# State-read stores in another shape, alpha's copy on another engine, three weight loads issued later, other warm-up counts and a new table of slots

## The chip, the cores and the metric

The kernel runs on one core of a Trainium2 chip. The metric is the device time of one execution in microseconds (us), less being better; the number given for a kernel is the median of several runs. A profile of one execution is taken beside them. Its span runs from the first to the last instruction that the profiler recorded, and the device time of that execution is a little longer than the span. The engines are called PE (TensorE), DVE (VectorE), ACT (ScalarE), POOL (GpSimd) and SP (SyncE); PEld is the weight load of TensorE.

## What is computed

Eight batches with eight heads each. A head has 512 tokens of width 64 (x) and 32 state rows of width 64. Tokens read from the state and the state reads from the tokens, and both results go through a feed-forward block with a sine activation.

```python
scores  = scale * x @ state.T            # 512 x 32 per head
a       = softmax(scores)                # over the state rows
xread   = a @ state                      # 512 x 64
scores2 = scale * state @ x.T            # 32 x 512
a2      = softmax(scores2)               # over the tokens
sread   = a2 @ x                         # 32 x 64
y       = concat([xread, sread])         # 544 rows per batch, heads side by side: 512 wide
h       = y @ w_in                       # 512 -> 2048
g       = h + sin(alpha * h)**2 / (alpha + 1e-9)
out     = g @ w_out                      # 2048 -> 512
```

All inputs and the output are fp32; the kernel multiplies in bf16.

## The kernel before

**Main idea.** The token reads are not formed. The kernel multiplies the state with w_in first (M, 256 rows of state and head by 2048), and then h is A times M, with A the normalised weights. One Exp serves both softmaxes: E = exp(scores), its row sums (R) normalise A, its column sums (C, made by a matmul with ones) normalise the state reads. The state reads of all eight batches are gathered in `xs_all`, 256 rows, and go through the feed-forward block as a ninth stage.

**Stages and slots.** The main loop has nine stages t (eight batches, then the state reads) of 16 slots f, one for each 128 columns of the 2048. A slot does, in this order: `mm1` (two matmuls of 512 columns into a PSUM buffer `h_ps`, then Sin on ACT, then the square s*s on POOL, or on DVE if the slot is listed in `SQ`); the PE work of the attention that the table puts there; `snake` of the slot two earlier on DVE (s2 / alpha + h, which makes `gT` and frees the PSUM buffer, of which there are four); the DVE squares that are due; some second matmuls `mm2` of the stage before, as many as `TWO0`, `TWO1` or `TWO` say; and then the work of other engines that the table puts there. So PE alternates between the first product of batch t and the second of batch t-1. When 16 second matmuls have filled a tile of 128 rows, ACT copies it out and SP stores it.

**The table.** `BATCH` says for batch 0, 1, 2 and all later ones in which slot each step of that batch's attention stands, counted from the start of the stage before its own (for M and W from its own stage): L the load of x, P the two packs of x, T its transpose, S scores, X Exp, R row sums, N the two scalings that make A, A its transpose, M the four quarters of M with `MA` saying whether ACT (1) or DVE (0) casts each half, W the state reads. `ND` lists which scalings run on DVE; others run on POOL. The order of the program is the order on each engine: nothing is reordered, and each engine waits in its own queue.

**Transposes.** For batches 0 and 1 PE transposes x and A (`T`, `AT_`) and DVE or ACT copies the result from PSUM. For later batches SP issues transposing DMAs (`T_dma`, `AT_dma`), which stand in SP's queue among the output stores.

**Start.** SP loads the state and the x of batch 0. POOL makes an identity, waits for the state (`held`), and then issues the casting loads: the four quarters of w_in ('i'), the four of w_out ('o') and the x of batch 1 in the order `LOADS`. PE runs `warm_up` matmuls, transposes the state (`prep_state`) and alpha (`prep_alpha`), and then goes through batch 0's attention: T, S, the first quarter of M (`m_step(0, 0)`), W and Cs, warm-ups again, and `AT_`.

**End.** The state reads of 256 rows give two output tiles. `store` writes a tile of state reads as 4 batches by 32 rows. The second tile is done in halves of 256 columns by `mm2_last`: ACT copies the first half, DVE the second, and each is stored on its own.

Of the kernel before, what the change touches and what calls it, by code (L numbers as in the profile page):

```python
# [12 lines left out]
BF16 = mybir.dt.bfloat16  # L13
# [6 lines left out]

BATCH = {0: {'M': (-11, 0, 6, 8), 'MA': ((1, 0), (1, 1), (1, 0), (1, 1))},
 1: {'P': (0, 1),
     'T': (3, 3),
     'S': (3, 3),
     'X': (3, 3),
     'R': (3, 7),
     'N': (8, 10),
     'A': 13,  # L30
     'M': (-6, 0, 3, 9),
     'MA': ((1, 1), (1, 1), (1, 1), (0, 1)),
     'W': (5, 5)},
 2: {'L': -8,
     'P': (-1, -1),
     'T': 1,
     'S': (6, 6),
     'X': (6, 6),
     'R': (7, 8),
     'N': (7, 11),  # L40
     'A': 11,
     'M': (-5, -2, 5, 10),
     'MA': ((1, 1), (1, 1), (1, 1), (0, 1)),
     'W': (-1, -1)},
 3: {'L': -18,
     'P': (-12, -11),
     'T': -6,
     'S': (2, 2),
     'X': (2, 2),
     'R': (3, 4),  # L50
     'N': (3, 9),
     'A': 12,
     'M': (-3, 1, 6, 8),
     'MA': ((1, 0), (1, 0), (0, 1), (1, 1)),
     'W': (-2, -2)}}

SQ = {0: (4, 8, 9, 11, 12, 15),
 1: (3, 6, 11, 12, 14),
 2: (0, 2, 5, 10, 11, 14),
 7: (0, 1, 2, 3, 4, 5, 8, 10, 12),  # L60
 8: (0, 1, 2, 3, 4, 8, 9, 11, 12, 14)}
ND = {1: (), 2: (0,), 3: (0,)}
XS0 = 0

TWO0 = (0, 0, 0, 0, 0, 4, 3, 1, 0, 0, 1, 6, 1, 2, 3, 0)
TWO1 = (2, 4, 2, 1, 1, 2, 3, 2, 5, 3, 9, 3, 0, 3, 3, 0)
TWO = (7, 3, 4, 7, 0, 6, 11, 5, 4, 1, 0, 6, 2, 4, 1, 3)
WARM = (8, 3)

LOADS = ('i0', 'i1', 'x1', 'i2', 'o0', 'o1', 'i3', 'o2', 'o3')  # L70


@with_exitstack
def kernel(
# [9 lines left out]
    nc = tc.nc  # L84

    B, H, S, D = x.shape
    Ns = state.shape[2]
    P = nc.NUM_PARTITIONS
    C = S // P
    Q = H // 2  # L90
    G = 2
    HH = H // G
    TB = S + Ns
# [7 lines left out]
    const = ctx.enter_context(tc.tile_pool(name="const", bufs=1))  # L101
# [35 lines left out]
    def load_x(b, parts):  # L137
        xnat = xpool.tile([P, H, C * D], BF16, name="xnat")
        xv = x[b].rearrange("h (p i) d -> p h (i d)", i=C)
        hs = H // parts  # L140
        for k in range(parts):
            nc.gpsimd.dma_start(
                xnat[:, k * hs:(k + 1) * hs, :], xv[:, k * hs:(k + 1) * hs, :]
            )
        xnat_l[b] = xnat
# [8 lines left out]
    w_in_sb = wpool.tile([P, Q, DFF], BF16, name="w_in_sb")  # L154
    w_in_v = moe_w_in.rearrange("(q p) f -> p q f", p=P)
    w_out_sb = wpool.tile([P, FT, DOUT], BF16, name="w_out_sb")
    w_out_v = moe_w_out.rearrange("(ft p) c -> p ft c", p=P)
    for what, k in LOADS:
        k = int(k)
        if what == "x":  # L160
            load_x(k, 1)
        elif what == "i":
            cols = slice(k * FW, (k + 1) * FW)
            nc.gpsimd.dma_start(w_in_sb[:, :, cols], w_in_v[:, :, cols])
        else:
            fts = slice(k * 4, (k + 1) * 4)
            nc.gpsimd.dma_start(w_out_sb[:, fts, :], w_out_v[:, fts, :])

    ones = const.tile([P, D], BF16, name="ones")
    nc.vector.memset(ones[:], 1.0)  # L170
# [5 lines left out]
    nc.vector.memset(stT[:].bitcast(U32), 0)  # L176
    alpha_sb = const.tile([P, FT], FP32, name="alpha_sb")
    inva_sb = const.tile([P, FT], FP32, name="inva_sb")
    xs_all = const.tile([P, Q, B * Ns], BF16, name="xs_all")

    def warm_up(n):
        if n:
            wp = psO.tile([P, S], FP32, name="o_ps", tag="o")
        for _ in range(n):
            nc.tensor.matmul(wp[:], warm[:, 0:P], warm[:], start=True, stop=True)

    def kind(t):
        return t if t < 2 or t >= B - 1 else 2


    def prep_state():
        st2 = const.tile([P, 16, 2, D], BF16, name="st2")
        for half, copy in ((0, nc.vector.tensor_copy), (1, nc.scalar.copy)):
            js = slice(half * 8, (half + 1) * 8)
            copy(st2[:, js], st_nat[:, js].unsqueeze(2).to_broadcast([P, 8, 2, D]))
        for half in range(2):
            tp = psH.tile([P, 8, P], BF16, name="st_ps", tag="h")
            for k in range(8):
                nc.tensor.transpose(
                    tp[:, k, :],  # L200
                    st2[:, half * 8 + k].rearrange("p r d -> p (r d)"),
                    ident[:],
                )
            for r in range(2):
                rows = slice(r * D, (r + 1) * D)
                src = tp[rows].rearrange("d k (e r2 jh) -> d e r2 jh k", r2=2, jh=2)
                dst = stT[rows].rearrange(
                    "d bg (h2 r2 jh hf k) -> d (bg h2) r2 jh hf k", h2=2, r2=2, jh=2, hf=2
                )
                nc.scalar.copy(dst[:, :, r, :, half, :], src[:, :, r])  # L210

    def prep_alpha():
        tp = psH.tile([P, FT], FP32, name="al_ps", tag="h")
        nc.tensor.transpose(tp[:], alpha_rows[:], ident_f[:])
        nc.vector.tensor_copy(alpha_sb[:], tp[:])


    class Att:
# [81 lines left out]
                    ALU.mult,  # L300
                )

        def AT_(a, gs, copy=nc.vector.tensor_copy):
            tp = psX.tile([P, len(gs), S], BF16, name="a_ps", tag="px")
            for k, g in enumerate(gs):
                for i in range(C):
                    nc.tensor.transpose(
                        tp[:, k, i * P:(i + 1) * P], a.A[:, g, i], ident[:]
                    )
            copy(a.AT[:, gs[0]:gs[-1] + 1, :], tp[:])  # L310

        def W(a, pool=psX, tag="px"):
            a.wc = pool.tile([P, Q, 3 * Ns], FP32, name="w_ps", tag=tag)
# [20 lines left out]
        def xs(a):  # L334
            rC = smallp.tile([P, Q, Ns], FP32, name="rC")
            nc.vector.reciprocal(rC[:], a.wc[:, :, 2 * Ns:])  # L336
            for r in range(2):
                rows = slice(r * D, (r + 1) * D)
                nc.vector.tensor_tensor(
                    xs_all[rows, :, a.b * Ns:(a.b + 1) * Ns],  # L340
                    a.wc[rows, :, r * Ns:(r + 1) * Ns],
                    rC[rows],
                    ALU.mult,
                )

# [29 lines left out]
    def mm1(t, f):  # L375
        n = S if t < B else B * Ns
        hp = psH.tile([P, S], FP32, name="h_ps", tag="h")
        if t < B:
            for g in range(G):
                nc.tensor.matmul(  # L380
                    hp[:, :n], Ms[t][:, g, f * P:(f + 1) * P], atts[t].AT[:, g, :],
                    start=(g == 0), stop=(g == G - 1),
                )
        else:
            for q in range(Q):
                nc.tensor.matmul(  # L386
                    hp[:, :n], w_in_sb[:, q, f * P:(f + 1) * P], xs_all[:, q, :],
                    start=(q == 0), stop=(q == Q - 1),
                )
        s = sinp.tile([P, S], BF16, name="s")  # L390
        nc.scalar.activation(s[:, :n], hp[:, :n], ACT.Sin, scale=alpha_sb[:, f:f + 1])  # L391
        s2 = sinp.tile([P, S], BF16, name="s2")
        if f in SQ[kind(t)]:
            late.append((s2, s, n))
        else:
            nc.gpsimd.tensor_tensor(s2[:, :n], s[:, :n], s[:, :n], ALU.mult)  # L396
        return hp, s2, n
# [26 lines left out]
    def store(t, st, o_sb, cols, eng):  # L424
        if t < B:
            r0 = t * TB + st
            eng.dma_start(out[r0:r0 + C * (P - 1) + 1:C, cols], o_sb[:, cols])
        else:
            n = P // Ns
            ov = out.rearrange("(b t) c -> b t c", t=TB)  # L430
            eng.dma_start(ov[st * n:(st + 1) * n, S:, cols], o_sb[:, cols])


    def mm2_last(t, st):
# [18 lines left out]

    warm_up(WARM[0])
    prep_state()
    prep_alpha()
    a = atts[0] = Att(0)
    a.alloc()
    a.pack(0)
    a.pack(1)  # L460
    a.T(0)
    a.T(1)
    a.S(0)
    a.X(0)
    a.S(1)
    a.X(1)
    a.Rs(0)
    a.N(0, nc.gpsimd)
    a.Rs(1)
    a.N(1, nc.vector)  # L470
    m_step(0, 0, (True, True))
    a.W(psO, "o")
    a.Cs()
    warm_up(WARM[1])
    nc.scalar.activation(tiny[:, 1:2], warm[:, 0:1], ACT.Sin)
    a.AT_([0], nc.scalar.copy)
    a.AT_([1])
    nc.vector.tensor_scalar(inva_sb[:], alpha_sb[:], 1e-9, None, op0=ALU.add)
    nc.vector.reciprocal(inva_sb[:], inva_sb[:])
# [15 lines left out]
    for b in range(B):  # L495
        p = BATCH[min(b, 3)]
        s0 = (b - 1) * FT
        if b > 1:
            add(post, s0 + p["L"], load_x, b, 1)
        if b:  # L500
# [8 lines left out]
            for g in range(G):  # L509
                add(pe, s0 + p["S"][g], att, b, "S", g)  # L510
                add(post, s0 + p["X"][g], att, b, "X", g)
                add(post, s0 + p["R"][g], att, b, "Rs", g)
                eng = nc.vector if g in ND[min(b, 3)] else nc.gpsimd
                add(post, s0 + p["N"][g], att, b, "N", g, eng)
# [17 lines left out]
    todo = [(0, st, ft, ft + 1) for ft in range(FT) for st in (0, 1)]  # L532
    rows(0, TWO0, todo)
    todo += [(0, st, ft, ft + 1) for st in (2, 3) for ft in range(FT)]
    rows(1, TWO1, todo)
    assert not todo
    for t in range(2, B + 1):
        todo = [(t - 1, st, ft, ft + 1) for st in range(C) for ft in range(FT)]
        rows(t, TWO if t < B - 1 else (4,) * FT, todo)

# [21 lines left out]
    n = B * Ns // P  # L562
# [31 lines left out]
```

## Time and profile before

The time before is 238.24 us, the median of 13 runs from 236.59 to 240.8 us. The profiled execution took 238.24 us as well.

| quantity | value |
|---|---|
| profiled execution, device time | 238.24 us |
| its span | 236.2 us |
| mean granted TensorE clock | 0.978 |
| PE busy | 216.6 us, 92% |
| DVE busy | 178.5 us, 76% |
| ACT busy | 163.2 us, 69% |
| POOL busy | 108.5 us, 46% |
| first `mm1` matmul starts | 16.79 us |
| last matmul ends | 229.0 us |

Busy time is the sum of instructions on an engine. For PE it includes the time a result needs to come out of the array, so that a PE that is busy need not be at its peak: one 512-column matmul of `mm1` is listed with 0.38 us, while one follows the other every 0.216 us. In the lists of groups, each row has a line of the kernel, an engine, an operation with its output and input, a count, and then busy time, the mean of one in ns, and the idle time of the engine before it with what ended it. The chain of waits is followed back from the last instruction, at each step to what released it.

### The profile page before, as it was taken

Reading aid. Unit: us, or ns where it says so; the run is one execution under the profiler, and the core shown is the slowest. Engines: PE = TensorE matmul, PEld = TensorE weight load, DVE = VectorE, ACT = ScalarE, POOL = GpSimd, SP = SyncE. Lnnn points to the kernel's source line nnn. Section 1 sums busy time; section 2 is a strip of 40 time slices with the busy share of each in tenths; the row PEclk is TensorE's granted clock in tenths of the full one; section 3 lists DMA queues with packets and bytes.
Section 4 is the critical chain, followed back from the end, with each engine's and each line's share of the span. In section 5 each row is a group of like instructions: output and inputs, shape, how many; then the busy total and the mean of one; then the engine's idle time right before and its main releaser. Section 6 shows DMA issues by size and latency. Waiting matters only on the chain.

```text
span 236.2 us, 4158 instructions
## 1 busy us (share of the span) xinstructions
PE 216.6 (92%) x1505; PEld 104.0 (44%) x1532; DVE 178.5 (76%) x315; ACT 163.2 (69%) x264; POOL 108.5 (46%) x116
## 2 busy tenths in 40 slices
PE   7587797899999999999999999999999999999970
PEld 2444242444544444444444344444444444656550
DVE  3669998998886989788988798788779876644300
ACT  4559976898796679767976597759776676554310
POOL 3936577538337634573358316731671044231200
PEclk9959999999999999999999999999999999999996
DMA  7999996807811781178119902710231111111211
GB/s 219 188 198 201 206 142 75 191 13 179 133 45 46 178 136 44 44 182 130 49 44 154 159 0 92 177 45 4 89 89 47 44 46 44 49 46 57 79 22 67
DMA packets 36578, 23.35 MB, mean 99 GB/s; under 512 B 19645, under 2 KB 32205, under 8 KB 36557
## 3 DMA queue, kind: packets, MB, share of 16 engines
q0 software_dynamic: 11504, 7.87, 23.7%
q1 hardware_dynamic: 25020, 15.21, 22.5%
q8 instruction: 12, 0.20, 0.3%
q14 instruction: 10, 0.07, 0.1%
q10 hardware_dynamic: 32, 0.01, 0.0%
HBM read 17.31 MB, written 8.91 MB: 111 GB/s over the span
## 4 chain that ended last, share of the span: by engine, by line
PE 75%; DMA 10%; DVE 7%; issue 2%; ACT 1%; POOL 1%; ACTq 0%
PE o_ps L415 44%; PE h_ps L380 19%; PE m_ps L361 4%; DMA xnat<-in_x_dram 3%; PE h_ps L386 3%; DMA w_in_sb<-in_moe_w_in_dram 3%; DVE gT L406 3%; DMA AT<-A 2%; DMA st_nat<-in_state_dram 2%; PE o_ps L440 1%; PE w_ps L316 1%; PE s_ps L271 1%; PE w_ps L327 1%; DVE xp L234 1%; DVE rC L336 1%
## 5 line engine op out<-in xcount | busy, mean ns | idle before, releaser
L396 POOL TENSOR_TENSOR s<-s 128x512 bf16<-128x512 bf16 (+1 forms) x84 | 85.4, 1023 | 109.5 <-ACT s L391 104.5
L415 PE MATMUL o_ps<-w_out_sb,gT 128*128 128x512 bf16 x508 | 130.7, 380 | 1.4 <-issue 0.8
L391 ACT ACTIVATE s<-h_ps,alpha_sb 128x512 bf16<-128x512 f32 (+1 forms) x144 | 93.8, 669 | 50.5 <-PE h_ps L380 37.1
L406 DVE SCALAR_TENSOR_TENSOR gT<-s,inva_sb,h_ps 128x512 bf16<-128x512 bf16 (+1 forms) x144 | 99.8, 712 | 21.8 <-POOL s L396 20.5
L380 PE MATMUL h_ps<-AT,M 128*128 128x512 bf16 x250 | 73.1, 381 | 4.3 <-DVE gT L406 2.7
L415 PEld LDWEIGHTS <-gT 128*128 128x128 bf16 x528 | 49.0, 98 | 57.0 <-issue 6.4
L380 PEld LDWEIGHTS <-M 128*128 128x128 bf16 x256 | 24.6, 98 | 34.0 <-issue 5.5
L403 DVE TENSOR_TENSOR s<-s 128x512 bf16<-128x512 bf16 (+1 forms) x60 | 25.5, 435 | 5.1 <-ACT s L391 4.8
L370 ACT CAST M<-m_ps 128x512 bf16<-128x512 f32 x46 | 25.5, 589 | 1.2 <-PE m_ps L361 1.2
L421 ACT COPY o_sb<-o_ps 128x512 f32<-128x512 f32 x33 | 19.6, 594 | 4.9 <-PE o_ps L415 4.7
L372 DVE CAST M<-m_ps 128x512 bf16<-128x512 f32 x18 | 12.3, 685 | 4.8 <-PE m_ps L361 4.8
L361 PE MATMUL m_ps<-w_in_sb,stT 64*32 64x512 bf16 x256 | 13.3, 393 | 1.5 <-DMA w_in_sb<-in_moe_w_in_dram 1.2
L284 DVE TENSOR_REDUCE R<-E 128x16 f32<-128x512 bf16 x16 | 10.9, 682 | 2.5 <-ACT E L280 2.5
L361 PEld LDWEIGHTS <-stT 64*32 64x32 bf16 x256 | 3.7, 89 | 14.8 <-issue 14.2
L280 ACT ACTIVATE E<-s_ps 128x512 bf16<-128x512 f32 x16 | 8.8, 595 | 1.9 <-PE s_ps L271 1.8
L234 DVE COPY xp<-xnat 128x1024 bf16<-128x1024 bf16 x14 | 9.1, 658 | 1.1 <-DMA xnat<-in_x_dram 1.1
L386 PE MATMUL h_ps<-xs_all,w_in_sb 128*128 128x256 bf16 x64 | 9.6, 273 | 0.0
L391 ACT ACT_TABLE_LOAD x7 | 9.0, 1283 | 0.1
L280 ACT ACT_TABLE_LOAD x7 | 9.0, 1283 | 0.1
L336 DVE RECIPROCAL rC<-w_ps 128x128 f32<-128x128 f32 x8 | 7.6, 949 | 1.0 <-PE w_ps L327 0.6
L386 PEld LDWEIGHTS <-w_in_sb 128*128 128x128 bf16 x64 | 6.3, 98 | 4.1
L295 POOL TENSOR_TENSOR A<-E,rR 128x512 bf16<-128x512 bf16 x7 | 7.3, 1047 | 0.0
(53 smaller groups left out, 98.1 us busy)
## 6 DMA issues: line engine op xcount, KB each, us to landing
out_dram<-o_sb SPq DMA_DIRECT2D x33, 256.0 KB, 2.3
xnat<-in_x_dram POOLq DMA_DIRECT2D x7, 512.0 KB, 6.3
w_in_sb<-in_moe_w_in_dram POOLq DMA_DIRECT2D x4, 512.0 KB, 10.6
w_out_sb<-in_moe_w_out_dram POOLq DMA_DIRECT2D x4, 512.0 KB, 17.9
x_first<-in_x_dram SPq DMA_DIRECT2D x2, 512.0 KB, 5.7
st_nat<-in_state_dram SPq DMA_DIRECT2D x1, 512.0 KB
out_dram<-o_sb SPq DMA_DIRECT2D x2, 128.0 KB
xT<-xp SPq DMA_TRANSPOSE x6, 3.9
```

The lines of the kernel that those rows point to most:

```text
L280: nc.scalar.activation(a.E[:, g], a.sp[g][:], ACT.Exp, scale=scale)
L361: nc.tensor.matmul(mp[g][o0:o0 + Ns, :], stT[rows, b * G + g, c0:c0 + Ns], w_in_sb[rows, 2 * g + h, fs * FW:(fs + 1) * FW], start=True, st ...
L370: nc.scalar.copy(dst, mp[g][:])
L372: nc.vector.tensor_copy(dst, mp[g][:])
L380: nc.tensor.matmul(hp[:, :n], Ms[t][:, g, f * P:(f + 1) * P], atts[t].AT[:, g, :], start=(g == 0), stop=(g == G - 1),)
L386: nc.tensor.matmul(hp[:, :n], w_in_sb[:, q, f * P:(f + 1) * P], xs_all[:, q, :], start=(q == 0), stop=(q == Q - 1),)
L391: nc.scalar.activation(s[:, :n], hp[:, :n], ACT.Sin, scale=alpha_sb[:, f:f + 1])
L396: nc.gpsimd.tensor_tensor(s2[:, :n], s[:, :n], s[:, :n], ALU.mult)
L403: nc.vector.tensor_tensor(s2[:, :n], s[:, :n], s[:, :n], ALU.mult)
L406: nc.vector.scalar_tensor_tensor(gT[t][:, f, :n], s2[:, :n], inva_sb[:, f:f + 1], hp[:, :n], ALU.mult, ALU.add)
L415: nc.tensor.matmul(op[:], gT[t][:, ft, st * P:(st + 1) * P], w_out_sb[:, ft, :], start=(ft == 0), stop=(ft == FT - 1),)
L421: nc.scalar.copy(o_sb[:], op[:])
```

## The change

It has these parts.

1. `store` writes a tile of state reads with two DMAs, one for the even and one for the odd state rows, the second always issued by ACT; each has 16 rows of the state as its slowest dimension, then 4 batches. `xs_all` is laid out so that rows of a tile come in this order (half of batches, state-row pair, batch, row within the pair), and `xs` and the ninth stage's `mm1` address it so.
2. `prep_alpha` copies alpha on ACT in place of DVE. The first `AT_` copy of batch 0 goes from ACT to DVE.
3. The last three loads of `LOADS` are issued by POOL behind its scaling of batch 0; the order of the loads changes.
4. `warm_up` is called with 9, 2, 1 and 1 matmuls in four places, where it was called with 8 and 3 in two.
5. `BATCH`, `SQ`, `ND`, `TWO0`, `TWO1` and `TWO` have new values. Among them: x is loaded one slot earlier for batch 2 and later batches; M of later batches is cast by ACT alone; both scalings of batches 3 to 7 are on DVE and both of batch 2 on POOL.

```diff
-BATCH = {0: {'M': (-11, 0, 6, 8), 'MA': ((1, 0), (1, 1), (1, 0), (1, 1))},
- 1: {'P': (0, 1),
+BATCH = {0: {'M': (-13, 0, 6, 7), 'MA': ((1, 0), (1, 1), (1, 0), (1, 1))},
+ 1: {'P': (1, 1),
      'T': (3, 3),
      'S': (3, 3),
      'X': (3, 3),
-     'R': (3, 7),
-     'N': (8, 10),
+     'R': (4, 6),
+     'N': (7, 10),
      'A': 13,
-     'M': (-6, 0, 3, 9),
+     'M': (-5, -2, 3, 9),
      'MA': ((1, 1), (1, 1), (1, 1), (0, 1)),
      'W': (5, 5)},
- 2: {'L': -8,
+ 2: {'L': -9,
      'P': (-1, -1),
      'T': 1,
      'S': (6, 6),
      'X': (6, 6),
-     'R': (7, 8),
+     'R': (7, 9),
      'N': (7, 11),
-     'A': 11,
-     'M': (-5, -2, 5, 10),
-     'MA': ((1, 1), (1, 1), (1, 1), (0, 1)),
+     'A': 14,
+     'M': (-5, -2, 6, 10),
+     'MA': ((1, 1), (0, 0), (1, 1), (0, 1)),
      'W': (-1, -1)},
- 3: {'L': -18,
-     'P': (-12, -11),
-     'T': -6,
+ 3: {'L': -19,
+     'P': (-12, -9),
+     'T': -9,
      'S': (2, 2),
      'X': (2, 2),
-     'R': (3, 4),
-     'N': (3, 9),
-     'A': 12,
-     'M': (-3, 1, 6, 8),
-     'MA': ((1, 0), (1, 0), (0, 1), (1, 1)),
-     'W': (-2, -2)}}
-
-SQ = {0: (4, 8, 9, 11, 12, 15),
- 1: (3, 6, 11, 12, 14),
- 2: (0, 2, 5, 10, 11, 14),
- 7: (0, 1, 2, 3, 4, 5, 8, 10, 12),
- 8: (0, 1, 2, 3, 4, 8, 9, 11, 12, 14)}
-ND = {1: (), 2: (0,), 3: (0,)}
+     'R': (4, 5),
+     'N': (4, 11),
+     'A': 11,
+     'M': (-3, 1, 4, 8),
+     'MA': ((1, 1), (1, 1), (1, 1), (1, 1)),
+     'W': (-1, -1)}}
+
+SQ = {0: (0, 4, 8, 9, 12, 15),
+ 1: (3, 5, 6, 7, 11),
+ 2: (2, 5, 7, 8, 9, 12, 15),
+ 7: (0, 5, 6, 11, 13, 15),
+ 8: (0, 1, 2, 3, 6, 9, 13, 15)}
+ND = {1: (), 2: (), 3: (0, 1)}
 XS0 = 0
 
-TWO0 = (0, 0, 0, 0, 0, 4, 3, 1, 0, 0, 1, 6, 1, 2, 3, 0)
-TWO1 = (2, 4, 2, 1, 1, 2, 3, 2, 5, 3, 9, 3, 0, 3, 3, 0)
-TWO = (7, 3, 4, 7, 0, 6, 11, 5, 4, 1, 0, 6, 2, 4, 1, 3)
-WARM = (8, 3)
-
-LOADS = ('i0', 'i1', 'x1', 'i2', 'o0', 'o1', 'i3', 'o2', 'o3')
+TWO0 = (0, 0, 0, 1, 3, 0, 3, 0, 0, 1, 2, 3, 2, 2, 2, 2)
+TWO1 = (2, 5, 3, 1, 1, 3, 3, 0, 3, 4, 9, 3, 0, 1, 4, 1)
+TWO = (3, 7, 3, 9, 2, 4, 9, 4, 2, 3, 1, 6, 3, 3, 2, 3)
+WARM = (9, 2, 1, 1)
+LATER = 6
+
+LOADS = ('i0', 'i1', 'x1', 'o0', 'i2', 'i3', 'o1', 'o2', 'o3')
...
-    for what, k in LOADS:
+
+    def load(what, k):
...
+    for w in LOADS[:LATER]:
+        load(*w)
...
-    xs_all = const.tile([P, Q, B * Ns], BF16, name="xs_all")
+
+    xs_all = const.tile([P, Q, B // 4, Ns // 2, 4, 2], BF16, name="xs_all")
...
-        nc.vector.tensor_copy(alpha_sb[:], tp[:])
+        nc.scalar.copy(alpha_sb[:], tp[:])
...
-        def AT_(a, gs, copy=nc.vector.tensor_copy):
+        def AT_(a, gs):
...
-            copy(a.AT[:, gs[0]:gs[-1] + 1, :], tp[:])
+            nc.vector.tensor_copy(a.AT[:, gs[0]:gs[-1] + 1, :], tp[:])
...
-                    xs_all[rows, :, a.b * Ns:(a.b + 1) * Ns],
-                    a.wc[rows, :, r * Ns:(r + 1) * Ns],
-                    rC[rows],
+                    xs_all[rows, :, a.b // 4, :, a.b % 4, :],
+                    a.wc[rows, :, r * Ns:(r + 1) * Ns].rearrange("p q (k l) -> p q k l", l=2),
+                    rC[rows].rearrange("p q (k l) -> p q k l", l=2),
...
-                    hp[:, :n], w_in_sb[:, q, f * P:(f + 1) * P], xs_all[:, q, :],
+                    hp[:, :n], w_in_sb[:, q, f * P:(f + 1) * P],
+                    xs_all[:, q].rearrange("p h k b l -> p (h k b l)"),
...
-            n = P // Ns
-            ov = out.rearrange("(b t) c -> b t c", t=TB)
-            eng.dma_start(ov[st * n:(st + 1) * n, S:, cols], o_sb[:, cols])
+            ov = out.rearrange("(b t) c -> b t c", t=TB)[st * 4:(st + 1) * 4, S:, cols]
+            for l, e in ((0, eng), (1, nc.scalar)):
+                e.dma_start(ov[:, l::2].rearrange("b k c -> k b c"), o_sb[l::2, cols])
...
     prep_alpha()
+    warm_up(WARM[1])
...
     a.T(1)
+    warm_up(WARM[2])
     a.S(0)
...
     a.N(0, nc.gpsimd)
+    for w in LOADS[LATER:]:
+        load(*w)
     a.Rs(1)
...
-    warm_up(WARM[1])
+    warm_up(WARM[3])
     nc.scalar.activation(tiny[:, 1:2], warm[:, 0:1], ACT.Sin)
-    a.AT_([0], nc.scalar.copy)
+    a.AT_([0])
```

## The prediction

> **What bounds the kernel now.** First the slices of the page, to see where TensorE is not full.
>
> ```profile
> PE   7587797899999999999999999999999999999970
> PEclk9959999999999999999999999999999999999996
> DMA  7999996807811781178119902710231111111211
> ```
>
> One digit is 5.9 us. TensorE is full from slice 8 (47 us) to slice 38; only the first eight slices and the last have gaps, and in slice 2 its clock was halved. So I cut the span at the first matmul of each batch (16.8, 35.5, 59.3 us and so on, from the timeline) and asked for the busy time of each engine by stage. The columns are length, then PE, PEld, DVE, ACT and POOL busy with counts, clock, DMA share and GB/s.
>
> ```profile
> 0.00:16.80 16.80, 11.93 (x100) 7.20 (x102) 9.07 (x15) 9.19 (x14) 9.76 (x18) 0.82 1.02 201
> 16.80:35.50 18.70, 16.00 (x122) 6.90 (x124) 17.63 (x34) 16.27 (x26) 12.09 (x12) 0.98 1.17 184
> 35.50:59.30 23.80, 21.65 (x179) 9.69 (x180) 21.59 (x37) 20.14 (x35) 14.25 (x14) 1.00 0.55 114
> 106.80:131.20 24.40, 23.53 (x166) 10.55 (x166) 21.07 (x37) 18.91 (x31) 12.81 (x13) 1.00 0.55 98
> 131.20:155.10 23.90, 23.50 (x165) 10.77 (x169) 19.95 (x34) 17.80 (x29) 11.26 (x11) 1.00 0.43 98
> 229.00:236.20 7.20, 0.00 (x0) 0.00 (x0) 0.42 (x1) 0.00 (x0) 0.00 (x0) 0.74 0.19 68
> ```
>
> A steady batch takes 23.9 us with PE busy 23.5: pure TensorE work, in which a slot moved on another engine is worth nothing. One batch took 24.4. Batches 0 and 1 leave PE idle 2.7 and 2.15 us, with DVE busy 94% and 91%. After the last matmul 7.2 us pass in which only one DVE copy runs. Then the chain, in order of time (start, length, what), for what ends those gaps:
>
> ```profile
> 5.13 6.96 DMA w_in_sb<-in_moe_w_in_dram
> ...
> 14.63 1.06 PE o_ps L185 x2
> 15.69 0.87 PE a_ps L307 x8
> ...
> 30.17 7.62 DMA xnat<-in_x_dram
> 37.85 1.11 issue
> ...
> 126.41 4.78 DMA AT<-A
> ```
>
> The first line is the first w_in quarter: no matmul of M starts before 12.1. Warm-up matmuls then stand ahead of the transposes of A. The x load of batch 2 holds DVE's pack until 37.8. The transposing DMA of A for batch 5 is the 0.5 us extra in the 24.4 us stage. Last the tail: SP's state-read stores and wait, then the DMA share in fortieths of the stretch 222 to 225.5 us (an ordinary 256 KB store) and of 228 to 235 us (the state-read stores), then the landing times of ordinary stores.
>
> ```profile
> 226.14 3.87 SPq L431 DMA_DIRECT2D out_dram<-o_sb  x3
> SPq L589 <- DMA out_dram<-o_sb: 4.8, 3, 2.2
> DMA  0000000000000000049999997100000000000000
> DMA  2313101221223222231222222222222222221100
> DMA to landing us min/median/max: 2.0/2.3/5.8
> ```
>
> The ordinary store fills nine tenths of the engines for about 0.65 us. The state-read stores hold them at two tenths until 234.5.
>
> **What the Trainium skill says.** "DMA: Bandwidth & Descriptors", section "Why a DMA increments its semaphore by 16 and not by 1": a DMA is spread over the largest number of engines, at most 16, that divides the slowest dimension of both its sides. The store of before has 4x32x512 against 128 partitions, so 4 engines; that of after has 16x4x512 against 64, so 16. The trace agrees for 4: a mean DMA share of 0.24 from 227.9 to 234.5 us. "TensorE: Matmul & The Clock Gate", section "What's actually happening": the clock is halved after an idle window of about 3.4 us and the windows do not start with the kernel. The trace agrees: clock 0.50 between 12 and 16 us, and warm-up matmuls 0.43 us apart there against 0.216 later. "SBUF — State Buffer", section "Who interferes with whom": a DVE operation with two SBUF inputs and a GpSimd operation reading SBUF exclude one another. The trace agrees:
>
> ```profile
> L292 DVE TENSOR_TENSOR A<-E,rR 128x512 bf16<-128x512 bf16 x6 | 4.2, 692 | 0.2
> L295 DVE TENSOR_TENSOR A<-E,rR 128x512 bf16<-128x512 bf16 x1 | 2.1, 2102 | 0.0
> L372 DVE CAST M<-m_ps 128x512 bf16<-128x512 f32 x18 | 12.3, 685 | 4.8 <-PE m_ps L361 4.8
> L370 ACT CAST M<-m_ps 128x512 bf16<-128x512 f32 x46 | 25.5, 589 | 1.2 <-PE m_ps L361 1.2
> ```
>
> The same scaling took 0.69 us, and 2.10 us where GpSimd's own scaling (13.13 to 14.20) fell into it.
>
> **Part by part**, against the profiled span of 236.2; 238.24 - 236.2 = 2.04 us lie around it, and 238.24 is also the median of the runs.
>
> *State-read stores.* The last DVE copy ends at 229.44 and the last issue starts at 229.47 (226.14 + 3.87, less its 0.54). SP's three waits from 230.07 on, 4.8 us with short gaps, end at 235.0; 1.2 us of closing follow. Afterwards the last 128 KB are two DMAs of 64 KB on 16 engines, issued by SP and ACT at once. An ordinary 256 KB lands 2.0 to 2.3 us after issue, of which 0.65 is data, so half of it lands at 229.5 + 1.7 to 2.0 = 231.2 to 231.5. The issue on ACT (0.42 for alpha's) stands behind ACT's copies and ahead only of the 0.37 us copy of the first half, 1.2 us of waiting before it. I take 231.5: **-3.5 us**, ends -2.8 (the odd partitions or ACT's queue slow it) and -3.8. The new layout of xs_all writes pairs of elements; I take the 0.29 us it costs now, because the operation reads fp32 from PSUM at the same count; at twice that, 0.6 us a batch of DVE, in stages where DVE is 80% busy.
>
> *Start.* The first w_in load stays first, behind the same state load, so M still begins at 12.1. Three warm-ups behind Cs become one: 2 x 0.43 = 0.85 us earlier for A's transposes. They must then have their inputs: GpSimd's scaling stood behind nine DMA issues until 13.13 and now stands behind six (the sixth ends at 10.06 now), so it starts when rR is there, about 11.3 to 11.7, and ends by 12.8; DVE's no longer meets it in full and ends near 13.4 instead of 14.75. Both AT copies are DVE's now (0.42 each), so AT is whole near 16.15 rather than 17.0: the first Sin moves from 17.74 to about 16.8. DVE goes on with inva, rC, xs and one square (0.42) taken from later. The pack of batch 1 then begins near 18.55 instead of 18.84. DVE being the fuller engine, I credit 0.3 + 0.42 = **-0.7**. The alpha copy (0.17) moves to ACT, which has 1.5 us idle before its first Exp; it frees DVE's pack from 7.44 to about 6.9, where the first x half lands (1.2 + 5.7), and that slack ends in the wait for w_in. The four added warm-ups, one at first, two and one between transposes, run while PE waits for DVE. If they keep the clock full through 12 to 17 us, M, W, Cs and the transposes halve and ACT's table load (to 15.17) sets the first Sin: then -2.3. If they hold up batch 0's transposes, +0.4.
>
> *Weight loads.* Behind each other in one queue they land about 2.6 us apart (the first at 12.1, the seventh at 27.9) until 33 (12.37 + 20.6), so issuing three of them later, at 12.8 to 15, costs nothing: the queue is behind by then. i3 lands one place earlier, and the 0.6 us wait of M's last quarter at 27.98 goes; ACT is next there. i2 and o1 land one place later, about 22.7 and 27.9; their first users stand near 24.5 and 29.5, a margin of 1.6.
>
> *Batches 0 and 1.* GpSimd's order ahead of x's load of batch 2 is unchanged (three squares, the scaling, the load), so the load moves with the stage and no more; the next x load comes one square earlier, away from batch 2's transpose (3.32 us issue now, 1.5 later). Two M casts move from batch 1's stage into batch 0's, 1.18 us of ACT (16.27 to 17.45 of 18.7). Two casts go from ACT to DVE (+1.37) and one scaling from DVE to GpSimd (-0.69) in batch 1's stage, where ACT sheds 2.36. Together I take **-0.4**, ends +0.7 and -1.6.
>
> *Steady batches.* Per batch ACT gains 3 casts (+1.77, 17.8 to 19.6 of 23.9), DVE loses 3 x 0.685, gains a scaling 0.69 and a square 0.42 (-0.95), and GpSimd loses two operations (-2.1). PE does the same work: 0, covered by PE itself. A's transpose is queued on SP behind the store of slot 11 and no longer behind x's transpose, now in slot 7. If it is issued near slot 12's start as now but without x's transposes, the 0.5 goes: **-0.5**. Ends: 0; and if DVE's second scaling is blocked to 2.1 us each time, A comes 1.4 us later where it has 0.9 to spare (issued at 151.01, 3.2 to landing, needed at 155.1): +0.5 x 5 = +2.5.
>
> Sum -3.5 - 0.7 - 0.4 - 0.5 = -5.1: span 231.1, time **233.1**.
>
> **Rivals.** *Clock held:* start -2.3 in place of -0.7, 231.5. For it: three more warm-ups lie in the 7 to 10.7 us window. Against: PE idles from about 10.5 to 12.1 anyway. *Stores do not gain:* if the wait is receipt rather than data, or the two queues meet, only 0.7 is won: 235.9. Against: two tenths for six microseconds. *Late A:* +2.5 instead of -0.5 gives 236.1; for it, the 2.10 row; against, GpSimd has fewer operations. *Slower, ACT takes the bound:* place, the steady stages; price, if ACT's idle (23.9 - 17.8 = 6.1) is latency it needs, a batch lasts 19.6 + 6.1 = 25.7, five times +1.8 = +9 less 5.1 gives 242; it decides once Sin runs later than four h buffers can cover, so a third of that gives 236.1 and seven tenths make it slower. Against it: after the two table loads with Exp (3.66 us) ACT recovers within five slots.
>
> **How the numbers follow.** Forecast 0.62, clock held 0.15, stores 0.08, late A 0.08, ACT 0.07. About 0.5% (1.2 us) is what the measurement tells from no change: 237.05 to 239.4. The first four end below that, with 0.03 of them taken off because two can meet; ACT is slower at its full price, no change at six tenths. So faster 0.90, same 0.05, slower 0.05. With the tail and batches 0 and 1 at their good ends together, -3.8 - 0.7 - 1.6 - 0.5 = -6.6 gives 231.6; at their bad ends, half of A's gain lost, -2.8 - 0.7 + 0.7 - 0.25 = -3.05 gives 235.2. Reaching out to clock held and to late A, the range is 230.4 to 236.2.
>
> **What would show it.** Right: the last wait of SP ends near 231.5 less the shift, DMA share near nine tenths for a moment after the last copy; first Sin near 16.8; stages of 23.9 us each. Wrong: a stage of batch 2 to 6 over 24.5 us with PE waiting for AT or for gT; clock 0.5 later than 17.5 us; PE waiting for w_in or w_out.

## The result, and the profile after

| | before | after |
|---|---|---|
| median of the runs, us | 237.61 (48 runs) | 233.09 (11 runs) |
| ratio of after to before | | 0.979, 95% interval 0.976 to 0.983 |
| profiled execution, device time, us | 238.24 | 231.60 |
| its span, us | 236.2 | 229.8 |
| mean granted TensorE clock | 0.978 | 0.992 |

A repeat of after, with its own runs of before beside it, gave 231.90 us and a ratio of 0.975 (0.970 to 0.979). The two medians are 4.5 us apart in the first comparison and 6.0 in the second (before 237.93 there). 5.1 were predicted. Some executions run longer than the rest of the same kernel at a lower clock, and the ratios leave these out while the medians keep them. The spans of the two profiled executions are 6.4 us apart, more than the medians, because the profiled execution of after was 1.5 us faster than its median and that of before 0.6 slower.

First the slices of the page of after, each 5.7 us.

```profile
PE   6697797999999999999999999999999999999992
PEclk9979999999999999999999999999999999999999
DMA  7999999264915371538044803610212111111112
```

TensorE is full from slice 7 on; before, from slice 8. The last slice is 2 tenths and belongs to the tail: in before it was 0, with a 7 in front of it. Next the same cut at the first matmul of a batch as was made of before; the columns are length, then PE, PEld, DVE, ACT and POOL busy with counts, clock, DMA share and GB/s.

```profile
0.00:14.85 14.85, 10.74 (x102) 6.45 (x103) 8.09 (x15) 8.77 (x14) 9.65 (x18) 0.89 0.96 198
14.85:33.95 19.10, 15.78 (x130) 7.09 (x133) 17.34 (x34) 17.20 (x28) 13.02 (x14) 1.00 1.27 203
33.95:56.70 22.75, 20.80 (x171) 9.43 (x172) 21.00 (x38) 18.45 (x30) 13.48 (x14) 1.00 0.65 119
104.10:127.90 23.80, 23.43 (x166) 10.69 (x168) 20.13 (x35) 19.86 (x32) 10.94 (x10) 1.00 0.44 100
127.90:151.80 23.90, 23.53 (x166) 10.73 (x168) 20.23 (x35) 19.86 (x32) 10.20 (x10) 1.00 0.44 99
225.66:229.80 4.14, 0.00 (x0) 0.00 (x0) 0.42 (x1) 0.00 (x0) 0.00 (x0) 0.97 0.20 59
```

The stretch after the last matmul fell from 7.2 to 4.1 us. The batch that took 24.4 us takes 23.8, and the one behind it 23.9 as before, though ACT has 19.86 us of work in it where it had 17.80. Behind the start, the largest loss is still in the first two batches, where PE idles 3.3 and 1.95 us.

To compare kernels by stage, I take the start of each stage's first Sin from the timeline. The stages that are not in the table (2, 3, 5, 6, 7) are equal within 0.1 us in all of these profiles. A stage's number is that of its batch, and the column "tail" runs from the last matmul to the end of the span.

| kernel (us) | first Sin | stage 0 | stage 1 | stage 2 begins | stage 4 | tail | span |
|---|---|---|---|---|---|---|---|
| before | 17.74 | 19.01 | 23.20 | 59.95 | 24.59 | 7.24 | 236.2 |
| before, repeated | 15.66 | 20.20 | 25.21 | 61.07 | 24.67 | 7.24 | 237.4 |
| after | 15.68 | 19.25 | 22.47 | 57.40 | 23.89 | 4.16 | 229.8 |
| after, repeated | 14.52 | 20.38 | 22.39 | 57.29 | 23.89 | 4.16 | 229.7 |

So the profile shows three gains: 3.1 us in the tail, 0.7 in stage 4, and 2.5 to 3.8 by the start of stage 2. The repeat of before also shows that its first Sin at 17.74 was an accident of one execution: it came at 15.66 in the other, and that bought nothing, because stage 0 took 1.2 us longer and stage 1 2.0. What happens in stage 1 is the main finding below.

The tail of after, first the timeline (start, length, engine, operation), then SP's last wait, then the DMA view of 222 to 229.8 us (share in fortieths, issues and us to landing):

```profile
222.81 3.88 SPq L438 DMA_DIRECT2D out_dram<-o_sb  x3
224.35 2.35 ACTq L438 DMA_DIRECT2D out_dram<-o_sb  x2
225.69 0.42 DVE L455 COPY o_sb<-o_ps 128x256 f32<-128x256 f32 x1 [6.17 <-PE o_ps L447]
```

```profile
SPq L600 <- DMA out_dram<-o_sb: 1.4, 1, 1.4
```

```profile
DMA  0000000000278992005871000003882000000000
...
out_dram<-o_sb SPq DMA_DIRECT2D x2, 64.0 KB, 2.0
out_dram<-o_sb ACTq DMA_DIRECT2D x2, 64.0 KB, 2.2
```

The last DVE copy ends at 226.11. SP's wait is 1.4 us where it was 4.8. The last stores fill 8 tenths of the engines for a moment, instead of two tenths for six microseconds.

### The profile page after: what moved, and what is told of

Read it like the earlier page. It is cut to its first block, busy times and chain, and to the rows that moved or that the text cites. A ratio compares the mean times of both kernels' runs of the same rounds, so it can differ in the third digit from the quotient of the medians.

```text
span 229.8 us, 4164 instructions
## 1 busy us (share of the span) xinstructions
PE 214.2 (93%) x1508; PEld 103.3 (45%) x1534; DVE 173.7 (76%) x306; ACT 169.3 (74%) x277; POOL 106.0 (46%) x112
## 4 chain that ended last, share of the span: by engine, by line
PE 82%; DMA 7%; DVE 5%; issue 2%; POOL 1%; ACT 1%; ACTq 0%
PE o_ps L422 47%; PE h_ps L386 21%; PE m_ps L367 4%; DMA xnat<-in_x_dram 3%; PE h_ps L392 3%; DMA w_in_sb<-in_moe_w_in_dram 2%; PE w_ps L322 2%; DMA st_nat<-in_state_dram 2%; PE o_ps L447 2%; PE s_ps L277 1%; PE w_ps L333 1%; DVE gT L413 1%; POOL s L403 1%; DVE xp L240 1%; DVE rC L342 1%
## 5 line engine op out<-in xcount | busy, mean ns | idle before, releaser
L422 PE MATMUL o_ps<-w_out_sb,gT 128*128 128x512 bf16 x506 | 132.7, 380 | 2.5 <-issue 1.7
L403 POOL TENSOR_TENSOR s<-s 128x512 bf16<-128x512 bf16 (+1 forms) x84 | 86.9, 1042 | 103.0 <-ACT s L398 101.6
L386 PE MATMUL h_ps<-AT,M 128*128 128x512 bf16 x252 | 74.7, 379 | 2.3 <-DVE gT L413 1.6
L422 PEld LDWEIGHTS <-gT 128*128 128x128 bf16 x528 | 48.5, 98 | 56.9 <-issue 6.6
L376 ACT CAST M<-m_ps 128x512 bf16<-128x512 f32 x59 | 31.7, 593 | 0.6 <-PE m_ps L367 0.6
L410 DVE TENSOR_TENSOR s<-s 128x512 bf16<-128x512 bf16 (+1 forms) x60 | 27.4, 463 | 5.8 <-ACT s L398 5.3
L428 ACT COPY o_sb<-o_ps 128x512 f32<-128x512 f32 x33 | 19.5, 592 | 9.8 <-PE o_ps L422 9.1
L240 DVE COPY xp<-xnat 128x1024 bf16<-128x1024 bf16 x14 | 6.7, 490 | 0.6 <-DMA xnat<-in_x_dram 0.6
L277 PE MATMUL s_ps<-stT,xT 128*128 128x64 bf16 x128 | 5.6, 194 | 1.4 <-DVE xT L255 1.2
L143 POOL DMA_DIRECT2D xnat<-in_x_dram x7 | 6.5, 933 | 0.0
```

Source lines behind the costliest of these rows:

```text
L376: nc.scalar.copy(dst, mp[g][:])
L386: nc.tensor.matmul(hp[:, :n], Ms[t][:, g, f * P:(f + 1) * P], atts[t].AT[:, g, :], start=(g == 0), stop=(g == G - 1),)
L410: nc.vector.tensor_tensor(s2[:, :n], s[:, :n], s[:, :n], ALU.mult)
L422: nc.tensor.matmul(op[:], gT[t][:, ft, st * P:(st + 1) * P], w_out_sb[:, ft, :], start=(ft == 0), stop=(ft == FT - 1),)
L428: nc.scalar.copy(o_sb[:], op[:])
```

## The experiments

Every median below stands beside runs of before on the same chip; "ratio" is that to before with its 95% interval. Changes are shown against the kernel that is named.

**The stores alone (e1) and all else (e2).** Before with after's `store` and `xs_all`, and after with those of before:

```diff
# e1, against before; e2 is the reverse of it, against after
-    xs_all = const.tile([P, Q, B * Ns], BF16, name="xs_all")
+    xs_all = const.tile([P, Q, B // 4, Ns // 2, 4, 2], BF16, name="xs_all")
...
-            eng.dma_start(ov[st * n:(st + 1) * n, S:, cols], o_sb[:, cols])
+            for l, e in ((0, eng), (1, nc.scalar)):
+                e.dma_start(ov[:, l::2].rearrange("b k c -> k b c"), o_sb[l::2, cols])
```

> The kernel before with the new layout of xs_all and the two-DMA state-read stores, nothing else. Theory (four engines held the last stores, sixteen do not): from the last DVE copy to the end of the span 4.1 us instead of 7.2, so the time falls by 3.0 us (2.6 to 3.5), ratio about 0.987. Rival (the stores gain little, the rest of the change brought it): it falls by 0.7 us or less, ratio 0.997 or more.

> The changed kernel with the stores and the layout of before. Theory: 3.0 us (2.6 to 3.5) above the changed kernel, 236.1 us, so 0.5 to 2 us below the kernel before; last copy to end of span 7.2 us. Rival: 0.7 us above the changed kernel.

Measured: e1 234.47 us, ratio 0.985 (0.980 to 0.991); e2 235.69 us, ratio 0.989 (0.985 to 0.993). Against 237.53 for before these are -3.1 and -1.8, and they add up to -4.9. The theory of e1 held (2.6 to 3.5 were expected), and the rival that the stores gain little fell. The stretch after the last matmul of e1, by its windows:

```profile
228.15:231.98 3.83, 0.00 (x1) 0.00 (x0) 0.42 (x1) 0.00 (x0) 0.00 (x0) 1.00 0.22 65
```

The tail goes from 7.24 to 3.82 us with before's table, and from 7.59 (e2) to 4.16 with after's. The stores therefore gain 3.4 us in both settings. The 0.35 us that after's table adds to the tail lies in the closing: from SP's first drain to the end of the span 0.8 us pass in before and e1, and 1.1 to 1.2 in e2, e5 and after. Why the table lengthens it was not found.

**Is it the engines or the second queue? (e3)** After with one DMA on SP for each piece, whose slowest dimension is 32 rows, so that 16 still divides it:

```diff
-    xs_all = const.tile([P, Q, B // 4, Ns // 2, 4, 2], BF16, name="xs_all")
+    xs_all = const.tile([P, Q, B // 4, Ns, 4], BF16, name="xs_all")
...
-            for l, e in ((0, eng), (1, nc.scalar)):
-                e.dma_start(ov[:, l::2].rearrange("b k c -> k b c"), o_sb[l::2, cols])
+            eng.dma_start(ov.rearrange("b j c -> j b c"), o_sb[:, cols])
```

> The changed kernel with one DMA per store, issued by SP alone, 32 state rows as the slowest dimension and 4 batches behind it, and a layout of xs_all to match. If the number of DMA engines is what counts, the tail is that of the changed kernel within 0.3 us. If the second queue is what counts, the tail is 1 us or more longer.

Measured: 232.83 us, ratio 0.977 (0.972 to 0.983), tail 4.11 us. The DMA view of 222 to 230 us in e3:

```profile
DMA  0000000000001999200079100000098000000000
...
out_dram<-o_sb SPq DMA_DIRECT2D x2, 128.0 KB, 2.0
```

One 128 KB store fills nine tenths of the engines and lands 2.0 us after issue, like two of 64 KB from two queues. So the second queue adds nothing. What e3 and after share, and before lacks, is a slowest dimension that 16 divides; the bytes are the same, and the DMA share of two tenths before and eight to nine tenths after fits 4 and 16 engines. That the second queue adds nothing agrees with the Trainium skill, "DMA: Bandwidth & Descriptors", section "Issuing engines are not separate DMA queues": DMAs from several engines end up on the same 16, and issuing from more than one saves only issue time.

**The start alone (e4).** Before's table and stores with after's warm-ups, load order, late loads and copies:

```diff
-WARM = (8, 3)
+WARM = (9, 2, 1, 1)
+LATER = 6
...
-LOADS = ('i0', 'i1', 'x1', 'i2', 'o0', 'o1', 'i3', 'o2', 'o3')
+LOADS = ('i0', 'i1', 'x1', 'o0', 'i2', 'i3', 'o1', 'o2', 'o3')
...
-        nc.vector.tensor_copy(alpha_sb[:], tp[:])
+        nc.scalar.copy(alpha_sb[:], tp[:])
```

> The kernel before with the start of the changed one (alpha on ACT, three loads behind batch 0's scaling, order of loads, warm-ups, both first AT copies on DVE) and the table and stores of before. Theory: the first Sin comes 0.9 us earlier at half clock and about 2 us earlier where the first w_in load lands early, and DVE passes on 0.7 to 2; time 0.7 to 2.0 us below before. Rival (the earlier start was an accident of one profiled execution): within 0.5 us of before.

Measured: 239.47 us, with runs from 235.11 to 247.39, and a ratio of 0.988 (0.980 to 0.996) that rests on only two of its six runs. Its profile, of the longest run, has three stretches at half clock, and PE waits 2.5 us for batch 2's transposed x (`xT`). So the run says little about the start, but it points at a place where before's table is fragile, and before was looked at again.

**Before, repeated (c0), and the table alone (e5).** e5 is before with after's `BATCH`, `SQ`, `ND`, `TWO0`, `TWO1` and `TWO`, as in the diff of the change, and nothing else.

> The kernel before once more, with another profile. If the early start of the changed kernel (first Sin 2.06 us earlier in its profile) is mostly an accident of the first profile of before (w_in landed at 12.1, half clock for 6.8 us), this profile shows the first M matmul near 11.2 and the first Sin near 16, as the kernel with the stores alone did. If the changed start brings it, this profile shows 12.1 and 17.7 again. The stage of batch 4 lasts 24.6 us in both cases, if A's late transpose belongs to the table of before.

> The kernel before with the changed tables (BATCH, SQ, ND, TWO0, TWO1, TWO) alone; start, order of loads and stores are those of before. Theory: the stage of batch 4 falls from 24.6 to 23.9 us, batches 0 and 1 together win 0 to 0.6 us, steady stages stay 23.9; time 0.7 to 1.3 us below before. Rival (ACT's added casts cost the steady stages something): a stage of batch 2 to 6 above 24.0 us.

Measured: c0 238.34 us, ratio 0.998 (0.993 to 1.002); e5 236.50 us, ratio 0.991 (0.987 to 0.995). The runs of c0 spread from 236.88 to 242.70 us, those of e5 only from 235.20 to 236.88. Stage 4 of e5 takes 23.89 us, so the table alone removes the longer stage, and no stage of batch 2 to 6 is above 24.0. Since e2 is e5 with the whole new start, the two also price the start: their ratios, 0.989 and 0.991, are 0.4 us apart, with intervals of about 0.9 us to each side. A gain of 0.7 us can be neither seen nor excluded by them. What c0's profile shows in stage 1: the wait of PE from 36 to 50 us, the transposing DMA with the load of x beside it (34 to 47 us), and four windows of 3.41 us.

```profile
PE s_ps L271 <- DMA xT<-xp: 2.1, 1, 2.1
```

```profile
xnat<-in_x_dram POOLq DMA_DIRECT2D x1, 512.0 KB, 6.8
...
xT<-xp SPq DMA_TRANSPOSE x1, 8.3
```

```profile
36.40:39.82 3.42, 3.08 (x21) 1.21 (x20) 3.38 (x6) 2.46 (x6) 3.08 (x4) 1.00 0.60 56
39.82:43.23 3.41, 3.41 (x42) 1.67 (x34) 2.15 (x4) 3.41 (x7) 1.66 (x3) 1.00 1.29 202
43.23:46.64 3.41, 1.23 (x20) 0.85 (x21) 3.30 (x7) 2.92 (x5) 1.04 (x1) 1.00 0.73 209
46.64:50.05 3.41, 3.41 (x10) 1.23 (x9) 3.34 (x8) 2.98 (x4) 1.01 (x1) 0.50 0.00 0
```

The transpose lands 8.3 us after issue. PE stands still for 2.1 us, has only 1.23 us of work in that window, and the next window runs at clock 0.50. Stage 1 is 2.2 us longer here than in e1 (25.21 against 23.01), whose transpose lands in 5.9 us and which has neither the wait nor a halved window there. The same DMA in after (DMA view of 32 to 45 us):

```profile
xnat<-in_x_dram POOLq DMA_DIRECT2D x1, 512.0 KB, 6.0
...
xT<-xp SPq DMA_TRANSPOSE x1, 3.8
```

What differs is how long before the transpose the load of batch 3's x was issued. All profiles, sorted by that distance:

| profile | x of batch 3 issued | transpose of batch 2 issued | between | transpose lands after |
|---|---|---|---|---|
| e9 | 33.12 | 38.28 | 5.16 | 3.8 |
| e2 | 32.94 | 38.09 | 5.15 | 3.8 |
| e8 | 33.03 | 37.22 | 4.19 | 3.9 |
| e3 | 33.09 | 37.27 | 4.18 | 4.0 |
| after | 33.06 | 37.12 | 4.06 | 3.8 |
| after, repeated | 33.03 | 37.03 | 4.00 | 4.1 |
| e7 | 32.96 | 35.77 | 2.81 | 5.4 |
| e5 | 36.10 | 38.77 | 2.67 | 5.7 |
| e6 | 36.03 | 38.69 | 2.66 | 5.6 |
| before | 36.74 | 39.40 | 2.66 | 5.5 |
| e1 | 36.02 | 38.39 | 2.37 | 5.9 |
| before, repeated | 35.84 | 37.07 | 1.23 | 8.3 |
| e10 | 35.95 | 37.15 | 1.20 | 8.6 |
| e4 | 37.62 | 38.32 | 0.70 | 9.4 |

The landing time follows the distance through 14 profiles with both tables: above 4 us about 3.9, at 2.7 about 5.6, near 1 more than 8. Seen from the load it is simpler still: wherever the distance is below 5 us, the transpose lands 1.8 to 2.8 us behind the landing of the load itself (1.8 in after, 2.1 in before, 2.8 in c0), as if it had to wait until the load was nearly through. PE waits for `xT` only in the last three. After's table issues the load one slot and one square earlier in POOL's queue. In before two things race, POOL's squares (ahead of the load) and the arrival of batch 2's x (ahead of the transpose), so an execution in which that x arrives earlier loses the gain again. That moving this one load alone would do the same was not tried. Nor is this the only way to lose the stage: in e9, where the distance is 5.16 us, PE waits 2.1 us for `gT` instead, the next window runs at half clock, and stage 1 takes 25.15 us.

**The transpose of x moved earlier (e10).** Before with one number changed, to see what makes stage 4 last 24.6 us:

```diff
  3: {'L': -18,
      'P': (-12, -11),
-     'T': -6,
+     'T': -9,
```

> The kernel before with one number changed: T of batches 3 and later -9 in place of -6, so that x's transposing DMA is issued some slots ahead of A's instead of directly before it. Theory: the stage of batch 4 falls from 24.6 to 23.9 us and A's transpose lands in 2.7 to 3.2 us in every batch; time 0.7 us below before. Rival (A is late because of its scaling on GpSimd, or the x load): 24.6 stays and one landing takes 4.8 us.

Measured: stage 4 takes 23.89 us, as in after. The median is 238.64 us, ratio 0.999 (0.995 to 1.003), so the 0.7 us that were expected cannot be seen in the time. That the scatter of stage 1 hides them, where this profile belongs to the last three of the table, is likely but not shown. One landing of A's transpose still took 4.2 us, where 2.7 to 3.2 were expected in every batch; it came in time. So the place of x's transpose alone removes the longer stage, though not all of the late landing.

**Parts of the start, each put back in after (e6, e7, e8, e9), and after repeated (c1).**

```diff
# e6
-WARM = (9, 2, 1, 1)
+WARM = (8, 0, 0, 3)
# e7
-LATER = 6
+LATER = 9
# e8: both; e9: both, and the one store of e3
```

> The changed kernel with warm-ups 8, 0, 0 and 3 as before. Theory: two more warm-ups ahead of A's transposes and no fewer in the wait; the first Sin 0.4 to 0.9 us later, time 0.2 to 0.9 us above the changed kernel. Rival (DVE and the x loads set batches 0 and 1, so the time of the first Sin does not reach the end): within 0.2 us of the changed kernel.

> The changed kernel with all nine loads issued ahead of batch 0's scaling. Theory: GpSimd starts its scaling 1.4 us later (near 13.1 instead of 11.75) and DVE's meets it again (2.1 instead of 0.9 us), so A's transposes and the first Sin come 0.7 to 1.4 us later; the loads land as before. Time 0.3 to 1.4 us above the changed kernel. Rival: the time of the first Sin does not reach the end, within 0.2 us.

> The changed kernel once more, with another profile, as the measure for the three beside it: 2.1% (1.7 to 2.5) below before; stages from batch 2 on 23.4, 23.9 and so on as in its first profile; batches 0 and 1 between 40 and 45 us together, by whether and where TensorE's clock is halved.

> The changed kernel with warm-ups 8, 0, 0 and 3 and all loads ahead of the scaling, so that of its start only the alpha copy, the AT copy and the order of the loads are left. Theory (neither part reaches the end): as the changed kernel or up to 1.2 us below it, as each of the two alone. Rival (each is worth something and stands in for the other): 1 us or more above the changed kernel.

> The same with one DMA per state-read store on SP alone. Theory: tail as with two DMAs (4.1 us from the last matmul to the end of the span) and time within 0.4 us of the kernel beside it.

| | median, us | ratio | first Sin | stage 2 begins |
|---|---|---|---|---|
| c1, after repeated | 231.90 | 0.975 (0.970 to 0.979) | 14.52 | 57.29 |
| e6 | 231.93 | 0.974 (0.968 to 0.979) | 14.74 | 59.14 |
| e7 | 231.86 | 0.975 (0.968 to 0.981) | 15.58 | 56.03 |
| e8 | 231.37 | 0.973 (0.967 to 0.979) | 15.64 | 57.49 |
| e9 | 231.88 | 0.973 (0.968 to 0.978) | 15.73 | 60.14 |

None differs from after, within intervals of 1.0 to 1.6 us to each side. In e6's profile the clock is halved from 19.5 to 26.3 us, behind a wait of PE of 2.1 us for the pack of batch 1's x, and that puts off its stage 2; the median shows no lasting loss. The warm-ups and the late loads are worth nothing that can be measured, and e8, with the lowest median, is not shown to beat after. The new order of the loads, alpha's copy on ACT and the copies on DVE were not taken back one by one. The chains of waits of after and of its repeat say why an earlier first Sin is not passed on (start, length, what). After first:

```profile
17.42 0.68 DVE xp L240 x2
18.12 0.75 DVE gT L413
...
25.12 2.04 POOL s L403 x2
27.16 0.19 POOL A L298
27.35 0.76 issue
28.10 7.37 DMA xnat<-in_x_dram
...
35.83 1.26 DVE xp L240
```

```profile
7.15 9.59 DMA xnat<-in_x_dram
16.76 1.61 DVE xp L240 x2
18.39 0.75 DVE gT L413
...
25.09 2.04 POOL s L403 x2
...
28.07 7.30 DMA xnat<-in_x_dram
...
35.74 1.26 DVE xp L240
```

The first Sin is 1.16 us earlier in the repeat, and the x of batch 2 is issued at the same time within 0.03 us; in e7 at 28.00, in e8 at 28.07. The lead is gone at the pack of batch 1's x. In the repeat DVE waits 0.5 us for this x, whose load was issued at 7.15 and lands at 16.74, and the pack then takes 1.61 us beside POOL's squares. In after the x has landed at 16.52, before DVE comes to it, and the pack takes 0.68. So the packs end at 18.37 and 18.10, and from there on the two executions are within 0.3 us of each other. The last quarter of w_in also keeps PE waiting, near 25.1. In after:

```profile
PE m_ps L367 <- DMA w_in_sb<-in_moe_w_in_dram: 1.0, 1, 1.0
```

But no chain of these four profiles passes through that wait. The stage 1 of e7 is 1.2 us shorter for another reason. Its chain:

```profile
28.00 6.95 DMA xnat<-in_x_dram
...
35.32 0.42 DVE xp L240
```

The load lands 0.4 us earlier, so the second half of the pack runs ahead of a square on POOL and takes 0.42 us instead of 1.26. The square on POOL begins at 35.69 in after, ahead of this half (35.83), and at 35.59 in e7, behind its start (35.32). The Trainium skill, "SBUF — State Buffer", section "Who interferes with whom", says that a DVE copy in a two-port mode and POOL shut one another out, and that whoever issues first has the ports for its whole instruction; the 1.26 against 0.42 us agree with that, though no view shows the mode of this copy. The 0.4 us by which the load landed earlier decide it, and the median of e7 shows no lasting gain.

## Why the prediction was right, and where it was not

- **State-read stores, -3.5: right.** 3.4 us in e1 and in e2. The working put the last landing 2.1 us behind the last copy; SP leaves its wait about 2.5 us behind it, and before took 5.9.
- **Start, -0.7: its path failed, and no gain was seen.** The first Sin did move, to 15.7 instead of 16.8, but so it does in before's own repeat, at 15.66. The 17.74 on which the step was built belonged to one execution, in which the first quarter of w_in came about a microsecond later and the clock was halved for 6.8 us. The part on GpSimd's scaling held: where the clock is full, late loads let DVE's scaling take 0.88 us and put the first Sin at 14.52 and 14.74 (c1, e6), and early loads make it 2.00 and 2.07 us with the first Sin at 15.58 and 15.64 (e7, e8). Late loads are not the only way to that, since the repeat of before has 0.89 us with early loads. What failed is "the pack of batch 1 then begins near 18.55": batch 1's x lands between 16.3 and 17.7 in the profiles, whatever the start does, and an earlier DVE waits for it. "Clock held" fell as a rival too: after has a half-clock stretch of 3.4 us from 11.1 on, and its repeat, which has none, is no faster.
- **Weight loads, 0: not tested whole, and partly wrong in the reason.** That the late issue costs nothing agrees with e7. "The 0.6 us wait of M's last quarter at 27.98 goes" did not happen. The load lands 2.4 us earlier (25.16 against 27.52 in the repeat of before), but the table asks for it about that much earlier, so PE waits 0.98 us where it waited 1.24. What the new order is for shows in e5, which has the new table with the old order: the table wants the first quarter of w_out in slot 3 instead of 5, and in e5 PE waits 1.9 us for it.
- **Batches 0 and 1, -0.4: mis-sized.** Against e1, where nothing collides, stages 0 and 1 together are 1.4 us shorter in after (43.09 to 41.72) and 0.3 in its repeat, and stage 2 begins 1.7 us earlier in both. Against the repeat of before the two stages are 3.7 us shorter (45.41). The working named the mechanism, "the next x load comes one square earlier, away from batch 2's transpose", and priced only SP's issue time (3.32 against 1.5). What it left out is the landing, 5.5 to 8.3 us against 3.8, the wait of PE, and the clock behind it. It was hidden in the one profile of before, where the distance was 2.66 us and PE just did not wait.
- **A's transpose, -0.5: right.** Stage 4 loses 0.7 us. e10 confirms that x's transpose has to leave slot 10 for it. The transposes of A land in 2.7 us each in the steady stages of after.
- **Steady batches, 0: right.** ACT has 19.86 us of work, 19.6 were predicted, and the stage stays at 23.9, so ACT does not become the bound. Late A fell too: DVE's second scaling takes 1.18 us at the median, against the 2.1 feared each time, and A is still in time. Line 298 is the first of the two, line 301 the second (ns least/median/most):

```profile
L298 DVE TENSOR_TENSOR A<-E,rR x5: 691/691/693, 64.0 to 159.6; 128x512 bf16<-128x512 bf16 x5
```

```profile
L301 DVE TENSOR_TENSOR A<-E,rR x6: 746/1181/1184, 12.5 to 169.7; 128x512 bf16<-128x512 bf16 x6
```

The sum came out near in part by luck: a start without a gain that can be seen and a batch 1 that gains more than was put down balance each other. By the medians of the experiments the parts are stores -3.1 us (e1), table -1.65 (e5), and for the start nothing that can be measured; by the ratios they are -3.5 and -2.2. The product of the two ratios, 0.985 and 0.991, is 0.976, between the two ratios of after.

## What to carry to other kernels

A store that ends a kernel should have a slowest dimension that 16 divides on both sides; the second queue is not needed for it (16 and 32 were tried here against 4). Before crediting an earlier start, follow it to the next arrival that it can't move, here the x of batch 1, in a queue that was full from the beginning. And of a transposing DMA ask how long before it a large load was issued: here 4 us were enough and 1 us cost over 4 us of landing, and a schedule in which this distance hangs on which queue is ahead scatters from run to run.

## What the runs showed of the hardware that was not expected

- A transposing DMA beside a casting load of x takes 3.8 to 4.1 us when it follows the load's issue by 4 us or more, and 8.3 to 9.4 when it follows by about 1. SP's issue of it then takes 4.8 to 5.8 us instead of 1.7 (after), which holds up the stores behind it: in c0 the next one is issued at 42.58, when it ends. Whether the cast or only the number of packets does this was not separated.
- The clock was halved after windows of 3.41 us that were far from idle. e9 and e4, by their windows:

```profile
36.76:40.17 3.41, 1.18 (x6) 0.38 (x5) 3.37 (x6) 0.52 (x1) 1.21 (x2) 1.00 0.90 143
40.17:43.58 3.41, 3.41 (x15) 0.89 (x16) 3.18 (x6) 2.73 (x6) 1.04 (x1) 0.50 0.69 188
```

```profile
135.87:139.28 3.41, 0.50 (x3) 0.26 (x4) 1.98 (x4) 0.41 (x1) 0.98 (x1) 1.00 1.13 111
139.28:142.69 3.41, 3.41 (x10) 1.07 (x8) 0.00 (x0) 0.69 (x1) 0.00 (x0) 0.50 0.52 120
```

PE was busy 1.18 and 0.50 us of 3.41 ahead of the halving, and 1.23 in c0. Counted in steps of 3.41 us from the end of an earlier halving, the emptiest windows of before (1.96 us busy, from 37.95) and of e2 (1.75, from 34.90) were not followed by one. PE's busy time alone does not draw the line, though: before's window from 7.24 was busy for 1.88 us, and half clock followed. So a gap of about two microseconds may cost nothing, or bring half clock for the next 3.41 us; that this hangs on how it falls into the windows fits these figures and was not tested. This goes with "TensorE: Matmul & The Clock Gate", section "What's actually happening", by which the windows run on their own; that a window still a third busy can be followed by half clock is what these runs add.
